# K by two queues, two batches in a nine-row layout, and paired 64-token tails in a linear-attention and expert kernel

## The chip, the cores and the metric

The kernel runs on one core of one Trainium2 chip. A time is the device time of one execution in microseconds (us); the figure quoted for a kernel is the median of its runs. A ratio is the mean time of one kernel's fast runs over that of the other's fast runs of the same rounds, so it is not quite the ratio of the two medians beside it.

Stage times below are taken from one profiled execution of each kernel. They locate a difference; whether a kernel is faster is decided by the timed runs.

## The reference

Eight batches of eight heads, 576 tokens, 64 values a head, all float32. The attention output becomes the 4608 x 512 input of a two-layer block.

```python
def phi(x):
    return np.where(x > 0, x, np.exp(x) - 1.0) + 1.0
q_p, k_p = phi(q), phi(k)
kv  = np.einsum('bhsd,bhse->bhde', k_p, v)
z   = np.sum(k_p, axis=2)
num = np.einsum('bhsd,bhde->bhse', q_p, kv)
den = np.einsum('bhsd,bhd->bhs', q_p, z)[..., None] + 1e-06
x   = (num / den) as (tokens, 512)
h   = x @ w_in                      # 512 -> 2048
g   = h / (1 + exp(-beta * h))
out = g @ w_out                     # 2048 -> 512
```

## The kernel before

TensorE's order is fixed by hand. A batch has an "h" stage (products with w_in), then a "y" stage (products with w_out), and the attention of a later batch is placed between those products. 576 tokens are four groups of 128 and a tail of 64; the eight tails are processed together as a ninth group at the end.

Batch 0 uses another layout: 64 partitions for heads 0 to 3, 64 for heads 4 to 7, nine tokens in each row, so it has no special tail. It is loaded by halves of the partitions:

```python
def load_nine(dst, src, h0=0, h1=HH, j0=0, j1=N9):
    for g in range(2):                       # one transfer for each half of the rows
        nc.gpsimd.dma_start(out=dst[g * TAIL : (g + 1) * TAIL, ...], in_=src[0, ...])
```

All other batches are loaded by a transfer to all 128 partitions, in packets of 512 bytes, and a small one for the tail:

```python
def load_rows(dst, src, b, eng=nc.gpsimd):
    eng.dma_start(out=dst[:, :, 0:NJ, :]..., in_=src[b, :, 0:MAIN, :]...)
    eng.dma_start(out=dst[0:TAIL, :, NJ, :], in_=src[b, :, MAIN:S, :]...)
```

GpSimd issues the transfers in program order; the order after w_in, and the y stage of batch 0:

```python
load_w_out(0); load_w_out(1)
load_k(1); load_q(1)
...                                          # attention of batch 0
load_w_out(2); load_v(1); load_w_out(3)
...
y_phase_wide(0, {
    4: [F(load_next, 3)],
    9: [F(kv_mm, 1), F(kv_evac, 1), F(w_out_scale, 3)],   # K^T V of batch 1
    10: [F(q_trans, 1, 0, 1, wide=True), F(q_trans, 1, 2, 3, wide=True)],
    11: [F(num_mm, 1, 0), F(num_norm, 1, 0)],
    ...                                      # cut
})
```

Later, Q of batch 2 is transposed by a DMA (`q_trans_dma(2)`).

## Time and profile before

| | before |
|---|---|
| time, median (3 runs) | 297.17 us (296.59 to 297.41) |
| profiled span | 295.1 us |
| TensorE busy | 283.9 us, 96% |
| y stage of batch 0, from its first product to the first of the next stage | 34.16 to 52.53 us: 18.37 |
| y stage of batch 1, likewise | 67.61 to 85.25 us: 17.64 |

A row of the timeline has the start, the busy time, engine, source line, operation, output and input, shapes and count; the bracket has the idle time just before and what ended it. A row of the stretches' table has the stretch and its length, busy time (and instruction count) of PE, PEld, DVE, ACT and POOL, then the granted TensorE clock (0.50 is half clock), the DMA share (the packets' own time over that of 16 engines) and GB/s. GB/s counts the bytes written. Of the names, vaug is V with columns of ones, kv_bd holds K^T V, q_pT is the transposed phi(Q), xs the normalized attention and xT its transpose. w_out lands as float32 in the space of xqk, xT and g, hence "xT<-in_moe_w_out_dram", and DVE then scales it. The prediction below shows the main lines of before. Its stretches while the weights and batch 1 are loaded:

```profile
28.00:32.00 4.00, 4.00 (x21) 1.75 (x18) 2.50 (x6) 2.75 (x4) 2.38 (x3) 1.00 1.50 205
...
40.00:44.00 4.00, 3.72 (x54) 1.89 (x54) 3.31 (x3) 2.99 (x3) 2.34 (x4) 1.00 1.21 321
```

And GpSimd's issue of the second transfer of V of batch 1 in its timeline:

```profile
30.20 0.89 POOL L76 DMA_DIRECT2D vraw<-in_v_dram  x1 [0.19 <-issue]
```

### The profile page before, as it was taken

Reading aid. Unit: us, or ns where it says so; the run is one execution under the profiler, and the core shown is the slowest. Engines: PE = TensorE matmul, PEld = TensorE weight load, DVE = VectorE, ACT = ScalarE, POOL = GpSimd, SP = SyncE. Lnnn points to the kernel's source line nnn. Section 1 sums busy time; section 2 is a strip of 40 time slices with the busy share of each in tenths; the row PEclk is TensorE's granted clock in tenths of the full one; section 3 lists DMA queues with packets and bytes.
Section 4 is the critical chain, followed back from the end, with each engine's and each line's share of the span. In section 5 each row is a group of like instructions: output and inputs, shape, how many; then the busy total and the mean of one; then the engine's idle time right before and its main releaser. Section 6 shows DMA issues by size and latency. Waiting matters only on the chain.

```text
span 295.1 us, 4750 instructions
## 1 busy us (share of the span) xinstructions
PE 283.9 (96%) x1891; PEld 143.9 (49%) x1912; DVE 124.0 (42%) x261; ACT 175.1 (59%) x234; POOL 52.7 (18%) x72
## 2 busy tenths in 40 slices
PE   8879999999999999999999999999999999999994
PEld 3557445644465544445444544454445444444444
DVE  4765488504365174616461646154715400110012
ACT  2788786889988780778087907790770077018500
POOL 8924474540003200330023000000000000000000
PEclk9999999999999999999999999999999999999999
DMA  7999999999637993699369945024502400120032
GB/s 103 196 207 343 256 272 192 256 193 192 89 142 100 175 131 113 130 174 154 98 129 159 159 109 124 2 71 116 127 0 72 118 36 0 38 90 16 0 73 71
DMA packets 72310, 37.09 MB, mean 126 GB/s; under 512 B 40912, under 2 KB 66784, under 8 KB 72288
## 3 DMA queue, kind: packets, MB, share of 16 engines
q0 software_dynamic: 38912, 20.45, 47.9%
q1 hardware_dynamic: 33216, 16.20, 22.9%
q8 instruction: 15, 0.25, 0.3%
q10 hardware_dynamic: 160, 0.13, 0.2%
q14 instruction: 7, 0.06, 0.1%
HBM read 36.71 MB, written 9.44 MB: 156 GB/s over the span
## 4 chain that ended last, share of the span: by engine, by line
PE 76%; DMA 9%; POOL 4%; ACT 4%; issue 4%; DVE 1%; ACTq 0%; POOLq 0%; DVEq 0%
PE mm L453 37%; PE mm L505 33%; DMA xT<-in_moe_w_out_dram 5%; DMA vraw<-in_v_dram 4%; PE att L399 3%; ACT e L229 2%; POOL xqk L131 1%; PE att L344 1%; PE mm L537 1%; POOL w_in L159 1%; ACT L229 1%; POOL vraw L131 1%; ACT g L445 1%; DVE qk_p L242 0%; POOL xqk L111 0%
## 5 line engine op out<-in xcount | busy, mean ns | idle before, releaser
L445 ACT ACTIVATE g<-mm,beta_c 128x512 bf16<-128x512 f32 (+2 forms) x156 | 97.3, 633 | 88.4 <-PE mm L453 88.1
L505 PE MATMUL mm<-w_out,g 128*128 128x512 bf16 x541 | 126.7, 379 | 1.2 <-issue 0.3
L453 PE MATMUL mm<-xT,w_in 128*128 128x512 bf16 (+2 forms) x560 | 108.1, 349 | 1.4 <-DMA w_in<-in_moe_w_in_dram 1.1
L453 PEld LDWEIGHTS <-w_in 128*128 128x128 bf16 x656 | 61.9, 98 | 62.4 <-DMA w_in<-in_moe_w_in_dram 1.2
L505 PEld LDWEIGHTS <-g 128*128 128x128 bf16 x560 | 53.0, 98 | 58.2
L515 DVE COPY y_sb<-mm 128x512 f32<-128x512 f32 x27 | 18.7, 691 | 70.6 <-PE mm L505 69.1
L229 ACT ACTIVATE e<-xqk 128x2560 bf16<-128x2560 bf16 x14 | 31.9, 2329 | 0.1
L415 DVE TENSOR_TENSOR xs<-att,rden 128x512 bf16<-128x512 f32 (+1 forms) x40 | 27.6, 689 | 1.4
L242 DVE TENSOR_TENSOR qk_p<-r,e 128x2560 bf16<-128x2560 bf16 x14 | 20.9, 1490 | 13.1 <-ACT e L229 12.4
L355 DVE CAST kv_bd<-att 64x130 bf16<-64x130 f32 x28 | 8.2, 292 | 32.2 <-PE att L344 31.8
L72 POOL DMA_DIRECT2D vraw<-in_v_dram x7 | 6.4, 909 | 84.2 <-DVE vaug L370 78.5
L413 DVE TENSOR_SCALAR den<-att 128x8 f32<-128x8 f32 (+1 forms) x40 | 6.5, 161 | 32.0 <-PE att L399 31.9
L399 PE MATMUL att<-kv_bd,q_pT 128*128 128x130 bf16 (+1 forms) x160 | 15.8, 221 | 1.1 <-DVE kv_bd L370 0.7
L399 PEld LDWEIGHTS <-q_pT 128*128 128x128 bf16 (+1 forms) x160 | 11.6, 100 | 10.7 <-DVE xs L415 2.4
L453 PE MATMUL mm<-xT_tail,w_in 128*128 128x512 bf16 x63 | 13.9, 379 | 0.1
L237 DVE TENSOR_SCALAR r<-xqk 128x2560 bf16<-128x2560 bf16 x14 | 11.6, 834 | 3.8 <-DMA xqk<-in_q_dram 2.3
L575 PE MATMUL mm<-g 128*128 128x512 bf16 x34 | 9.9, 452 | 1.2 <-DVE g L143 1.2
L229 ACT ACT_TABLE_LOAD x7 | 9.0, 1283 | 0.1
L414 DVE RECIPROCAL rden<-den 128x8 f32<-128x8 f32 (+1 forms) x40 | 8.1, 202 | 1.4
L72 POOL DMA_DIRECT2D xqk<-in_k_dram x7 | 6.9, 984 | 6.3 <-DMA w_in<-in_moe_w_in_dram 2.8
L76 POOL DMA_DIRECT2D xqk<-in_k_dram x7 | 7.4, 1057 | 1.5 <-DMA w_in<-in_moe_w_in_dram 1.3
L256 ACT ACTIVATE e<-xqk 128x1280 bf16<-128x1280 bf16 (+1 forms) x4 | 4.4, 1155 | 5.4 <-DMA xqk<-in_k_dram 5.3
(71 smaller groups left out, 140.0 us busy)
## 6 DMA issues: line engine op xcount, KB each, us to landing
out_dram<-y_sb SPq DMA_DIRECT2D x28, 256.0 KB, 2.3
xqk<-in_k_dram POOLq DMA_DIRECT2D x7, 512.0 KB, 10.7
xqk<-in_q_dram POOLq DMA_DIRECT2D x7, 512.0 KB, 11.3
vraw<-in_v_dram POOLq DMA_DIRECT2D x7, 512.0 KB, 11.3
w_in<-in_moe_w_in_dram POOLq DMA_DIRECT2D x4, 512.0 KB, 11.0
g<-in_moe_w_out_dram POOLq DMA_DIRECT2D x4, 512.0 KB, 10.9
out_dram<-y_sb SPq DMA_DIRECT2D x14, 128.0 KB, 5.2
xqk<-in_moe_w_out_dram POOLq DMA_DIRECT2D x2, 512.0 KB, 14.4
```

Source lines behind the costliest of these rows:

```text
L72: eng.dma_start(out=dst[:, :, 0:NJ, :].rearrange("p h j d -> p h (j d)"), in_=src[b, :, 0:MAIN, :].rearrange("h (p j) d -> p h (j d)", j=NJ),)
L229: nc.scalar.activation(st[b, "e", a][:, h0:h1], xqk[b % NX][:, a, h0:h1], ACTF.Exp)
L237: nc.vector.tensor_scalar(st[b, "r", a][:, h0:h1], xqk[b % NX][:, a, h0:h1], 0.0, 1.0, ALU.max, ALU.add)
L242: nc.vector.tensor_tensor(st[b, "p"][:, a].rearrange("p j (h d) -> p h j d", h=H)[:, h0:h1], st[b, "r", a][:, h0:h1], st[b, "e", a][:, h0: ...
L355: nc.vector.tensor_copy(kv_bd[b % 2][i][gs, :, g, :], st[b, "kvp"][gs, 2 * i : 2 * i + 2, :])
L399: nc.tensor.matmul(nps[:n, p // 2, c0 : c0 + 2 * (D + 1)], st[b, "qT"][:, t, p, :n], kv_bd[b % 2][p // 2][:, p % 2], start=True, stop=True ...
L415: nc.vector.tensor_mul(xs[:n], nv[:, :, :, 0:D], rden[:n, :, :, None].to_broadcast([n, 2, 4, D]))
L445: nc.scalar.activation(g_sb[b % 2][:, ff, c0:c1], hp[:, c0:c1], ACTF.Silu, scale=beta_c[:, ff : ff + 1],)
L453: nc.tensor.matmul(hp[:, c0:c1], w_in_sb[ff // 4][:, kc, (ff % 4) * P : (ff % 4 + 1) * P], x[:, t0:t1, kc, :] if b < B else x[:, kc, c0:c1 ...
L505: nc.tensor.matmul(yp, g_sb[b % 2][:, ff, t * P : (t + 1) * P], w_out_sb[ff // 4][:, ff % 4, :], start=(ff == 0), stop=(ff == FC - 1),)
L515: nc.vector.tensor_copy(y_sb, yp)
L575: nc.tensor.matmul(st["warm"], g_sb[0][:, FC - 1, 0:P], g_sb[0][:, FC - 1, :], start=True, stop=True, skip_group_check=True,)
```

## The change

The intent: bring the first K sooner by letting SP issue a part of it (as float32, into space that is free by then); give batch 1 the nine-row layout as well, so that batches 0 and 1 have no tails inside the attention; multiply the tails of two batches in one step, each on one half of TensorE's columns; and transpose all tails of x by DMA rather than by TensorE. The core of the diff:

```diff
-    load_nine(k9, k)
-    load_nine(q9, q, j1=4)
+    load_nine(k_last, k, 0, KF, N9, eng=nc.sync)          # K, columns 5 to 8, float32
+    load_nine(x9[0][1][:, :, 0:KF], k, 0, 0, KF)
+    load_nine(x9[0][0][:, :, 0:QF], q, 0, 0, QF)
 ...
-    load_k(1)
-    load_q(1)
+    load_nine(x9[1][1], k, 1)
+    load_nine(x9[1][0], q, 1)
 ...
-    load_v(1)
+    load_nine(v9[1], v, 1)
 ...
     def num_mm(b, t):
-            nc.tensor.matmul(nps[:n, ...], st[b, "qT"][:, t, p, :n], kv_bd[b % 2]...)
+            for i in range(1 if t < NJ else 2):
+                bb, n, r0 = (b, P, 0) if t < NJ else (b - 1 + i, TAIL, i * TAIL)
+                nc.tensor.matmul(nps[r0 : r0 + n, ...], st[bb, "qT"]..., kv_bd[bb % 2]...)
 ...
-        if by_dma(b):
+        if by_dma(b) or t == NJ:
             nc.sync.dma_start_transpose(out=x_dst(b, t), in_=xs...)
 ...
-    warm(10); beta_trans(); make_beta(); warm(20)
+    warm(10); beta_trans(); warm(15)                        # make_beta later
 ...
-        9: [F(kv_mm, 1), F(kv_evac, 1), F(w_out_scale, 3)],
+        9: [F(kv1), F(w_out_scale, 3)],                     # nine-row form of the same
 ...                                                         # cut: batch 2's x copies to DVE, stores
```

## The prediction

> **What bounds the kernel now.** I read the page's totals first, then a table of the stages, then the timeline inside the stages. The stages are cut where TensorE changes from products with w_in ("h") to products with w_out ("y"). In this table the first number after the stretch is its length, the second is TensorE's busy time, and GB/s is what all DMA engines moved.
>
> ```profile
> PE 283.9 (96%) x1891; PEld 143.9 (49%) x1912; DVE 124.0 (42%) x261; ACT 175.1 (59%) x234; POOL 52.7 (18%) x72
> ...
> 0.00:17.16 17.16, 13.23 (x143) 6.42 (x144) 11.11 (x35) 9.60 (x13) 13.02 (x26) 1.00 1.06 157
> 17.16:33.94 16.78, 16.35 (x151) 11.21 (x152) 9.54 (x23) 13.87 (x32) 7.93 (x10) 1.00 1.28 263
> 33.94:52.53 18.59, 17.64 (x147) 9.42 (x149) 13.86 (x29) 13.69 (x15) 10.69 (x13) 1.00 1.43 249
> 52.53:67.60 15.07, 15.07 (x97) 8.62 (x96) 3.39 (x7) 13.11 (x22) 6.95 (x6) 1.00 1.48 224
> 67.60:85.25 17.65, 16.31 (x126) 8.14 (x128) 7.90 (x18) 17.00 (x17) 0.00 (x0) 1.00 0.89 135
> 85.25:101.41 16.16, 16.16 (x138) 9.36 (x137) 7.86 (x13) 12.66 (x24) 4.69 (x6) 1.00 0.93 137
> 101.41:116.50 15.09, 14.98 (x83) 7.34 (x84) 7.16 (x18) 7.80 (x5) 0.00 (x0) 1.00 0.87 142
> 235.80:263.40 27.60, 27.50 (x127) 12.50 (x128) 2.77 (x4) 10.99 (x16) 0.00 (x0) 1.00 0.10 39
> ```
>
> The row 235.80:263.40 holds nothing but 128 products of 512 columns (one record is missing): 27.60/128 = 0.2156 us each, the full pace. Nine groups of 512 tokens cost 9 x 27.6 = 248 us, which the change doesn't touch. What is left of 295.1 us is 47: 17.2 us of start, about 3.8 at the end, and some 26 of attention products and gaps inside the stages. TensorE's own order is the bound from 17 us on; DVE and ACT matter only where they open a gap in it. So each stage's worth is "its products at full pace, plus gaps". A y stage has 13.8 us of main products. The stages at 33.94 and 67.60 take 18.59 and 17.65, so that is where gaps are.
>
> The timeline shows them, each with what ended it:
>
> ```profile
> 7.49 3.16 ACT L256 ACTIVATE e<-xqk 128x1280 bf16<-128x1280 bf16 x3 [5.25 <-DMA xqk<-in_k_dram]
> ...
> 17.16 1.07 PE L453 MATMUL mm<-xT,w_in 128*128 128x128 bf16 x16 [1.10 <-DMA w_in<-in_moe_w_in_dram]
> ...
> 43.23 0.82 PE L344 MATMUL att<-vaug,qk_p 128*64 128x65 bf16 x40 [0.28 <-DVE vaug L370]
> ...
> 45.75 0.62 PE L380 MATMUL att<-identity,qk_p 128*128 128x128 bf16 x8 [0.28 <-DVE kv_bd L355]
> ...
> 79.33 0.41 PE L399 MATMUL att<-kv_bd,q_pT 128*128 128x130 bf16 x4 [0.34 <-DMA q_pT<-qk_p]
> ...
> 83.07 0.38 PE L433 MATMUL att<-identity,xs 128*128 128x128 bf16 x4 [0.61 <-ACT xT L372]
> ...
> 140.70 0.25 PEld L399 LDWEIGHTS <-q_pT 128*64 128x64 bf16 x4 [0.42 <-DVE xs L415]
> 140.70 0.42 PE L399 MATMUL att<-kv_bd,q_pT 128*64 128x130 bf16 x4
> 141.05 4.86 PEld L505 LDWEIGHTS <-g 128*128 128x128 bf16 x24
> ```
>
> See that K arrives at 7.5; that the first h product waits 1.1 us for w_in, not for x, whose copy (DVE, 15.88 for 0.42 us) ended at 16.30; that batch 1 waits for V and for bank release, batch 2 for an ACT copy; and that a 64-token tail holds TensorE from 140.70 to 141.05, 0.35 us, where a full group of 128 tokens takes 0.23 (138.65 to 138.88).
>
> **What the skill says.** (1) "DMA: Bandwidth & Descriptors", section "Issuing engines are not separate DMA queues": transfers from different issuers share the same 16 engines, and a second issuer saves only issue time. The trace agrees for 4 us on: the share is 1.15 and more there. But K's first packet starts at 2.73, while the beta row's, issued on SP, starts at 1.82 (packet records), so SP can fill an idle 0.9 us. (2) Same page, "SWDGE vs HWDGE vs iDMA": a cast needs GpSimd's queue, so the SP part of K arrives as f32. (3) "VectorE: DVE Perf Modes", "The perf-mode tier table": tensor_scalar is half as fast from f32 SBUF as from bf16. The trace agrees: 128x512 from f32 took 0.44 us, 128x2560 from bf16 0.83. (4) "TensorEngine Tiling (Array Packing)", "Performance Considerations": columns up to 64 permit two halves. The trace's 40 products of 128*64 by 65 columns occupy 43.23 to 43.98 = 19 ns each, against 65/512 x 0.2156 = 27 ns for a lone one: halves do overlap.
>
> **The change, part by part.** Counts of TensorE instructions are from both programs' instruction order.
>
> K by two queues. Per packet, K's 1152-byte writes took a median 107 ns (512 packets, 32 per engine: 3.4 us from 2.73); 640-byte ones 69 ns (2.2 us); SP's own 1024-byte output packets about 46 ns (1.5 us). New: SP starts at about 1.85, does 0.9 us alone, its last 0.6 interleaves, so K's engine time ends at 2.73 + 2.2 + 0.6 = 5.5 in place of 6.1 (an estimate; the slowest engine lags a further 1 us in both). Everything queued behind, w_in too, comes 0.6 earlier. x gains the same less 0.2 us for the f32 relu and still precedes w_in; beta's five small DVE operations (1.1 us) move into a wait for TensorE (1.5 us at 11.4 to 12.9). First h product at about 16.55: **-0.6**.
>
> Stage 17.16 (h of batch 0): its tail products (0.35) and its four 64-wide transposes (0.22) go: **-0.57**.
>
> Stage 33.94 (y of 0, attention of 1): K^T V in 36 products of 64 rows by 130 columns in place of 40; their like at L307 took 1.19 us for 36 of 128 columns, so about 1.05 against 0.75, +0.3. Q's transposes become 32 of 64x64 (16 took 0.41 with drain; about 0.75 against 0.9), -0.15. V of batch 1 comes in 512 packets of 1152 bytes in place of 1024 of 512 and 512 of 128: 3.4 us per tensor in place of 4.9 (64 x 60 + 32 x 32 ns per engine); K, Q and V of batch 1 together 4 us earlier, so the waits of 0.28 at 43.23 (V) and, with Q's banks taken as one tile, 0.28 + 0.2 at 45.75 go; of 1.6 us of gaps I keep 0.9, because the second product of the group now waits for three ACT copies (2.2 us). Net **-0.5**.
>
> Stage 52.53 (h of 1): tail products now 8, for both batches; at half overlap 0.45 against 0.35; transposes of the tail (0.22) go to DMA: **-0.15**.
>
> Stage 67.60 (y of 1, attention of 2): the x copies go from ACT to DVE, which is 45% busy there, and the second transposes move four products later. The gap at 83.07 (0.61 by the row, 0.78 between neighbours' ends) goes, that at 79.33 stays: **-0.8**.
>
> Stage 85.25 (h of 2): tail products and transposes go (0.57), and a part of the small gaps beside them: **-0.7**.
>
> Batches 3 to 7: tails of 4 and 6 vanish (0.35 + 0.09 before each: -0.88); 3, 5 and 7 do pairs (+0.1 each): **-0.6**.
>
> Sum: 0.6 + 0.57 + 0.5 + 0.15 + 0.8 + 0.7 + 0.6 = 3.9. 297.17 - 3.9 = **293.2 us**. The end (last store at 290) is the same work.
>
> **Rivals.** (a) The two column halves do not overlap when the weights differ per batch: then a pair costs 0.70, four pairs lose 4 x 0.25, and the time is 294.2. For it: each 64-column product costs 88 ns where a full one costs 58, so a weight load shows. Against it: the 19 ns above. (b) K's two queues only share: DMA is saturated from 3.5 us, packets rise by 512, and the fixed part of a packet, some 24 ns, costs 512 x 24/16 = 0.77 us, as much as the early start gives. Then the start gains nothing and the result is 293.8. For it: share over 1. Against: SP's packets are shorter than GpSimd's of like size. (c) In the stage at 33.94 DVE becomes the bound: it gets a memset pair of 0.75 us (0.48 + 0.27) before the kv copies and more ones to set; together some 0.95 us. If phi of Q isn't early, the products at 47.07 wait up to 0.7 longer: 293.9. (d) The other way: an early V lets all gaps of that stage close and w_in's slowest engine (last packet 1 us behind the mean) gains from K's part without GpSimd's ring: 1.5 us more, 291.7.
>
> **Range and chances.** Losses (a) to (c) all together give 295.3; gain (d) 291.7, with the 0.2 us spread of runs. 8 in 10: 291.5 to 295.1. Faster by 2% needs 291.2 or less, 6 us of gain where I can point at 3.9 and (d)'s 1.5: 0.08. Slower by 2% has no mechanism here: 0.01.
>
> **What would show it.** Right: first exp near 6.9 and first h product near 16.5, still waiting for w_in; no TensorE wait for V in batch 1; the wait for an ACT copy of xT gone; pairs of tails occupying 0.4 to 0.5 us; the steady y stage of even batches at 14.7, odd ones at 15.2. Wrong: a pair at 0.7 us (a), first h product still at 17.1 (b), TensorE waiting for kv_bd or xs of batch 1 longer than before (c). The prediction fails if the start moves over 1.5 us, or the stages at 33.94 and 67.60 keep their gaps.

## More of the kernel before

Experiments were timed in four sittings (on chips that the record numbers 15, 11, 11 and 14), each with its own runs of the kernel before, whose medians were 296.4 to 296.7 us. Ratios, not medians, are compared across sittings.

## The result, and the profile after

| | before | after |
|---|---|---|
| time, median (4 runs each) | 296.96 us (296.59 to 297.41) | 298.38 us (298.27 to 298.58) |
| ratio of fast runs | | 1.0048 (95%: 1.0031 to 1.0065) |
| profiled span | 295.1 | 296.5 |

The change is half a per cent slower, where a gain of 3.9 us was predicted: "within 2%", as predicted, but outside the range. The stage table of the changed kernel, with cuts at the same places as in the prediction's table of before:

```profile
0.00:16.43 16.43, 12.78 (x138) 6.23 (x140) 9.25 (x30) 8.98 (x12) 14.09 (x27) 1.00 1.10 176
16.43:32.63 16.20, 15.77 (x143) 10.97 (x143) 7.47 (x20) 13.96 (x32) 4.45 (x8) 1.00 1.17 267
32.63:56.48 23.85, 19.31 (x160) 9.78 (x162) 15.45 (x35) 13.33 (x16) 12.69 (x16) 0.93 1.35 225
56.48:71.34 14.86, 14.86 (x97) 8.53 (x96) 3.46 (x7) 12.91 (x21) 4.64 (x6) 1.00 1.45 222
71.34:88.17 16.83, 16.30 (x126) 8.10 (x128) 8.60 (x20) 15.91 (x15) 0.00 (x0) 1.00 0.83 97
88.17:103.55 15.38, 15.38 (x130) 9.00 (x130) 7.68 (x12) 11.67 (x21) 4.69 (x6) 1.00 1.01 163
```

Every row but the third is shorter than its partner before. The third, the y stage of batch 0 with batch 1's attention, is 23.85 us where it was 18.59. It is also the only one whose clock is not 1.00.

The start of each stage, from TensorE's first product in it:

| stage starts at | before | after | change within the stage before it | predicted |
|---|---|---|---|---|
| h of 0 | 17.16 | 16.43 | -0.73 | -0.6 |
| y of 0 | 34.16 | 32.85 | -0.58 | -0.57 |
| h of 1 | 52.53 | 56.48 | **+5.26** | -0.5 |
| y of 1 | 67.61 | 71.35 | -0.21 | -0.15 |
| h of 2 | 85.25 | 88.17 | -0.82 | -0.8 |
| y of 2 | 101.19 | 103.33 | -0.78 | -0.7 |
| end | 295.08 | 296.50 | -0.72 | -0.6 |

So one stage took all the gain and 1.4 us more. TensorE's timeline in that stage, with a pair of tails (112.98) from later on:

```profile
45.76 1.21 PE L342 MATMUL att<-vaug,qk_p 64*128 64x130 bf16 x36 [3.25 <-DVE vaug L362]
47.12 1.35 PE L548 MATMUL mm<-w_out,g 128*128 128x512 bf16 x3 [0.16 <-issue]
...
49.38 1.66 PE L548 MATMUL mm<-w_out,g 128*128 128x512 bf16 x4
...
112.98 0.42 PE L440 MATMUL att<-kv_bd,q_pT 128*64 128x130 bf16 x8
113.33 5.35 PE L548 MATMUL mm<-w_out,g 128*128 128x512 bf16 x24
```

TensorE stood for 3.25 us waiting for the copy of V of batch 1, against 0.28 before. Right after it, three products of 512 columns took 1.35 us and four took 1.66, about twice the 0.2156 each: the clock record has half clock from 47.25 to 50.67 us. A wait of 0.70 us for w_out at 40.62 adds to it. The pair of tails holds TensorE from 112.98 to 113.33, 0.35 us, as long as a single tail did.

DVE's timeline says why V was late:

```profile
32.07 0.88 DVE L214 TENSOR_SCALAR w_out<-xT,rbeta 128x512 bf16<-128x512 f32 x2 [1.99 <-DMA xT<-in_moe_w_out_dram]
...
44.94 0.76 DVE L362 COPY vaug<-vraw 128x2304 bf16<-128x2304 bf16 x1 [0.77 <-DMA vraw<-in_v_dram]
```

V is copied at 44.94 where it was 41.91, and w_out's second quarter is scaled at 32.07 where it was 29.94; both waited for a transfer. The chain of waits links the two:

```profile
13.94 18.11 DMA xT<-in_moe_w_out_dram
32.33 12.51 DMA vraw<-in_v_dram
```

The second half of V is issued only when that quarter of w_out has landed:

```profile
32.33 0.77 POOL L136 DMA_DIRECT2D vraw<-in_v_dram  x1 [2.10 <-DMA xT<-in_moe_w_out_dram]
```

In both kernels GpSimd's rows show the same habit: it issues a transfer once the one eight places before it has landed. Before, that cost V's second transfer no wait on a DMA (0.19, issue); now it cost 2.10 us. So the question is why a transfer of w_out, which the change doesn't touch, lands 2 us later. In the packet records, its last 4096-byte packets (after 28.3 us) took 165 to 172 ns each before, and 256 to 472 ns now. Meanwhile the stream as a whole:

```profile
28.00:32.00 4.00, 4.00 (x21) 1.78 (x19) 1.08 (x3) 2.61 (x5) 1.10 (x2) 1.00 1.22 200
...
40.00:44.00 4.00, 1.89 (x8) 0.68 (x7) 2.87 (x5) 1.59 (x3) 2.00 (x2) 1.00 1.07 270
```

At 28 to 32 us, while K and Q of batch 1 are loaded, it moves as many bytes as before (200 against 205 GB/s), at a smaller share (1.22 against 1.50). In the mixed stretch at 40 it moves 270 where it was 321.

### The profile page after: what moved, and what is told of

It reads as the page before. It is cut to its first block, busy times and chain, and to the rows that moved or that the text cites. A ratio compares the mean times of both kernels' runs of the same rounds, so it can differ in the third digit from the quotient of the medians.

```text
span 296.5 us, 4735 instructions
## 1 busy us (share of the span) xinstructions
PE 282.6 (95%) x1886; PEld 143.0 (48%) x1907; DVE 120.4 (41%) x254; ACT 171.9 (58%) x227; POOL 50.0 (17%) x72
## 4 chain that ended last, share of the span: by engine, by line
PE 82%; DMA 10%; POOL 4%; DVE 2%; issue 1%; POOLq 0%; DVEq 0%
PE mm L548 37%; PE mm L494 36%; DMA xT<-in_moe_w_out_dram 6%; DMA vraw<-in_v_dram 4%; PE att L440 3%; PE att L382 2%; POOL xqk L136 1%; PE mm L580 1%; PE att L494 1%; POOL w_in L161 1%; POOL vraw L136 1%; DVE xs L456 1%; POOL xqk L111 0%; PE att L342 0%; PE att L295 0%
## 5 line engine op out<-in xcount | busy, mean ns | idle before, releaser
L231 ACT ACTIVATE e<-xqk 128x2560 bf16<-128x2560 bf16 x12 | 27.4, 2328 | 0.1
L456 DVE TENSOR_TENSOR xs<-att,rden 128x512 bf16<-128x512 f32 x36 | 24.9, 692 | 1.2
L244 DVE TENSOR_TENSOR qk_p<-r,e 128x2560 bf16<-128x2560 bf16 x12 | 17.9, 1493 | 12.8 <-ACT e L231 12.1
L454 DVE TENSOR_SCALAR den<-att 128x8 f32<-128x8 f32 x36 | 5.9, 163 | 27.7 <-PE att L440 27.5
L440 PE MATMUL att<-kv_bd,q_pT 128*128 128x130 bf16 (+1 forms) x160 | 14.1, 221 | 0.7 <-DVE kv_bd L408 0.4
L268 ACT ACTIVATE e<-xqk 128x1280 bf16<-128x1280 bf16 (+2 forms) x5 | 7.7, 1562 | 5.4 <-DMA xqk<-in_k_dram 5.4
L410 ACT ACTIVATE q_pT<-att 128x512 bf16<-128x512 bf16 (+2 forms) x8 | 4.9, 652 | 9.1 <-PE att L295 9.1
L239 DVE TENSOR_SCALAR r<-xqk 128x2560 bf16<-128x2560 bf16 x12 | 9.7, 819 | 0.0
L455 DVE RECIPROCAL rden<-den 128x8 f32<-128x8 f32 x36 | 7.3, 203 | 1.2
L494 PE MATMUL att<-xT,w_in 128*128 128x512 bf16 x32 | 7.2, 379 | 0.0
```

Of the source, the lines that this page charges most:

```text
L231: nc.scalar.activation(st[b, "e", a][:, h0:h1], xqk[b % NX][:, a, h0:h1], ACTF.Exp)
L239: nc.vector.tensor_scalar(st[b, "r", a][:, h0:h1], xqk[b % NX][:, a, h0:h1], 0.0, 1.0, ALU.max, ALU.add)
L244: nc.vector.tensor_tensor(st[b, "p"][:, a].rearrange("p j (h d) -> p h j d", h=H)[:, h0:h1], st[b, "r", a][:, h0:h1], st[b, "e", a][:, h0: ...
L268: nc.scalar.activation(st[b, "e", a][:, j0:j1].rearrange("p j h d -> p h j d"), in9(b, a, j0, j1), ACTF.Exp,)
L440: nc.tensor.matmul(nps[r0 : r0 + n, p // 2, c0 : c0 + 2 * (D + 1)], st[bb, "qT"][:, t, p, :n], kv_bd[bb % 2][p // 2][:, p % 2], start=True ...
L455: nc.vector.reciprocal(rden[:n], den[:n])
```

## The experiments

The first theory was that batch 1's nine-row layout, by its transfers, makes V late, and that V's lateness is the whole loss. Rivals were the half clock, K's two queues, and the order of V and w_out.

### Batch 1 in the layout of before

The rest of the change stays.

```diff
-    load_nine(x9[1][1], k, 1); load_nine(x9[1][0], q, 1)
+    load_k(1); load_q(1)
-    load_nine(v9[1], v, 1)
+    load_v(1)
     # and exp, relu, phi, K^T V, Q's transposes and stores of batch 1 as before
```

> Only batch 1 is put back to the 128-partition layout with its 64-row tails; K by two queues, batch 0 without a tail, paired tails and DMA transposes stay. Theory T1 (the 64-partition loads of batch 1 slow the DMA stream): V of batch 1 lands near 41.5 us again in place of 44.9, TensorE's 3.25 us wait before batch 1's K^T V shrinks to 1.3 or less, the clock does not fall to half, and the time is 293 to 294.5 us. Theory T2 (the early f32 K on SP, or the issue order, is what delays V): V still lands near 44 and the time stays within 0.7 us of 298.4.

Measured: 298.0 us (296.26 to 298.13), ratio 1.0040 (1.001 to 1.007). TensorE's timeline:

```profile
42.55 0.82 PE L384 MATMUL att<-vaug,qk_p 128*64 128x65 bf16 x40 [1.15 <-DVE vaug L410]
...
81.54 0.62 PE L442 MATMUL att<-kv_bd,q_pT 128*128 128x130 bf16 x4 [3.43 <-DMA q_pT<-qk_p]
81.95 1.91 PE L550 MATMUL mm<-w_out,g 128*128 128x512 bf16 x4
```

V came back to 41.67 us, and the h stage of batch 1 starts at 51.86, 4.6 us before the changed kernel. Half of the theory holds. But the time hardly moved, because a second wait appeared in the next stage: TensorE stood 3.43 us for the transposed Q of batch 2 and then ran at half clock for 3.41 us (four products in 1.91). So V's lateness had hidden another loss. The first row shows a third thing: V lands when it landed before the change (41.67 against 41.91), so TensorE, which comes earlier, waits longer (1.15 against 0.28). The 1.5 us gained up to the y stage's start shrink to 0.67 at the next.

### Work for TensorE during the wait

```diff
         kvp = att_banks()
+        st["warm"] = kvp[:, 0]
+        warm(14)                    # fourteen idle products while V comes
         kv_mm9(...)
```

> The changed kernel with 14 filler products of 512 columns (14 x 0.216 = 3.0 us) put where TensorE waits for V of batch 1. If the 3.41 us at half clock that the trace shows after that wait is due to the idleness, the clock stays at 1.00 and the time falls by about half of 3.4 us, to 296.7 us; the wait itself stays. If the half clock has another cause, the time stays at 298.4 or gets worse.

Measured: 298.3 us, ratio 1.0071 (1.0048 to 1.0094). The half clock at 47 us was gone (in the profiled run it now lay at 11.76 to 15.17), and K^T V started at 45.60 instead of 45.76. One of its runs had a mean clock of 1.000 and still took 298.36, where 296.7 was expected. The stage became 1 us shorter in the profile (33.61 to 56.22), but only because it began 0.76 us later; it ended 0.26 earlier. Taking the half clock at 47 us away doesn't bring the time back.

The traces show why. From the start of K^T V to the next stage TensorE needs 9.30 us in the kernel before and 10.72 in the changed kernel; here, at full clock, it still needs 10.62. Three other runs with batch 1 in the nine-row layout and no half clock there (K by one queue, and both runs with four transfers of 64 rows, below) need 10.71 or 10.72. At full clock TensorE waits for DVE instead; DVE's timeline, then TensorE's:

```profile
46.87 0.48 DVE L92 MEMSET xqk<- 64x512 uint32 x1 [0.16 <-issue]
```

```profile
51.26 0.38 PE L548 MATMUL mm<-w_out,g 128*128 128x512 bf16 x1 [0.33 <-DVE w_out L214]
...
52.42 0.40 PE L474 MATMUL att<-identity,xs 128*128 128x128 bf16 x4 [0.56 <-DVE xs L456]
```

In the nine-row layout DVE clears tail rows (two memsets, 0.48 and 0.27 us) before it copies K^T V, so that copy starts 2.04 us after K^T V where it was 1.26, and all that follows on DVE is later. So some 1.4 us of the loss come with the nine-row layout, whatever the clock does, and the waits point to its work on DVE. No run takes the memsets away alone, so that cause is argued, not shown.

### K by one queue

```diff
-    load_nine(k_last, k, 0, KF, N9, eng=nc.sync)
-    load_nine(x9[0][1][:, :, 0:KF], k, 0, 0, KF)
+    load_nine(x9[0][1], k, 0)                # and the beta row goes back to SP
```

> The changed kernel with K of batch 0 by GpSimd's queue alone again. If two queues are worth the 0.7 us by which the first h product came earlier (16.43 against 17.16), that product goes back to about 17.1; and as the wait for V of batch 1 is set by the same DMA stream, V lands some 0.4 us later and the time is 298.6 to 299.2. If K's two queues are themselves what delays V (T2), V lands earlier than 44.9 and the time falls below 298.

Measured: 297.92 us, ratio 1.0051 (1.0032 to 1.0071), the same as the whole change. Whether K comes by two queues makes no difference that these runs can see. V's copy began at 44.19 us, 0.75 earlier, and the median is a little under 298, which by the letter are T2's signs; but the ratio has not moved (1.0051 against 1.0048), and V is still 2.3 us later than before. The first h product came at 17.12, as expected, but in this profile a half-clock window (12.60 to 16.01) lay ahead of it. TensorE still waited 2.83 us for V (45.01 us), here without a half-clock window after it.

### V ahead of a quarter of w_out

```diff
-    load_w_out(2)
     load_nine(v9[1], v, 1)
+    load_w_out(2)
     load_w_out(3)
```

> The changed kernel with V of batch 1 issued before the third quarter of w_out. T1 with a stream bound by its rate: V lands near 40 and that quarter near 44 in place of 41.6, so TensorE waits for w_out instead (it reaches it at 39.9) and the time changes by less than 1 us. If only V's place in the queue was wrong, the time falls by 3 us or more.

Measured: 298.53 us, ratio 1.0066 (1.0045 to 1.0087).

```profile
42.92 3.22 PE L548 MATMUL mm<-w_out,g 128*128 128x512 bf16 x8 [1.97 <-DVE w_out L214]
46.78 1.21 PE L342 MATMUL att<-vaug,qk_p 64*128 64x130 bf16 x36 [0.64 <-DVE vaug L362]
```

The wait for V fell to 0.64 us and that for w_out rose to 1.97. V itself landed at about 41 us (its last packet ended at 40.67), near the 40 that was expected; its copy stood behind the scaling of w_out in DVE's order until 45.80. The order only chooses who waits.

### The rows of a transfer: a failed try

The Trainium skill, "SBUF — State Buffer", section "Door 1: The DMA port swizzle (why [64,N] ≈ [32,N])", says that a transfer to 64 partitions reaches 8 of the memory's 16 ports. The next two runs were to tell this from the packet's length. The first has transfers to all 128 rows, the second has as many transfers to 64 rows.

```diff
+    for h in range(HH):                       # run 1: one head of each half, 128 rows
+        nc.gpsimd.dma_start(out=dst[:, h]..., in_=src[b].rearrange("(g h) (p j) d -> h g p (j d)", ...)[h])
```

> The changed kernel, but K, Q and V of batch 1 come in four transfers each that write 1152-byte packets to all 128 partitions (one head of each half a transfer), in place of two transfers each to 64 partitions. Same bytes, same packets, same layout. Theory A (transfers to 64 partitions use the memory badly, so the stream slows and V is late): V of batch 1 lands near 42 us, TensorE's wait for it falls from 3.25 us to under 1.3, the first h product of batch 1 starts at 52 to 53.5 instead of 56.5. Theory B (the 1152-byte packets, or the number of transfers allowed under way, make V late): V still lands at 44 to 46 us or later, since there are now more transfers of which each must wait for the one eight before it, and the wait stays above 2.5 us.

> The control of the run before: K, Q and V of batch 1 in four transfers each as there, of the same 1152-byte packets and the same bytes, but each to 64 partitions (two heads of one half). Theory A (64 partitions): V lands at 44.5 us or later as in the changed kernel, TensorE waits 3 us or more, and this run is slower than the other. Theory B (packets or number of transfers): this run and the other agree within 0.5 us in V's landing.

Measured: 304.26 us for the 128 rows (ratio 1.0303, 1.0225 to 1.0380) and 296.75 for the 64 (1.0006, 0.9982 to 1.0030). In the first, TensorE waited 2.15 us for w_out and 5.83 for V; in the second V's copy began at 42.86 and the wait was 1.55 us. Read as they were written, both expectations are against the theory of the rows (the second's Theory B failed too: V's copies were 7 us apart). But the first run is no test. Its stream moved 110 GB/s at 28 to 30 us, and some 1460 packets of 4 bytes ran from 28 to 29 us, where other runs have at most some twenty in a microsecond. Its source pattern has the two halves as the outermost dimension. The skill, "DMA: Bandwidth & Descriptors", section "Rules for kernel authors", says that an outermost dimension shorter than 16 confines a transfer to at most as many engines. No record here names a packet's engine, so that stays a probable cause. What the second run shows is that four smaller transfers in place of two, which alternate between the halves, halve the wait. It also shows that V's late issue is not by itself what makes V late. GpSimd's timeline in the second run:

```profile
33.60 2.52 POOL L146 DMA_DIRECT2D vraw<-in_v_dram  x4
```

All of V was issued there after the changed kernel had issued its last part (32.33), and V still came 2.1 us earlier (42.86 against 44.94).

### Shorter packets to 64 rows

```diff
-    load_nine(x9[1][1], k, 1)
+    load_nine(x9[1][1][:, :, 0:4], k, 1, 0, 4)       # 512-byte packets
+    load_nine(x9[1][1][:, :, 4:N9], k, 1, 4, N9)     # 640-byte packets; Q and V likewise
```

> The changed kernel, but K, Q and V of batch 1 come in packets of 512 and 640 bytes (token columns 0 to 3, then 4 to 8), four transfers a tensor to 64 partitions each, in place of 1152-byte packets. Same bytes, layout and rows. The run with four transfers of 1152-byte packets to 64 partitions is its control: there V's copy began at 42.86 us, TensorE waited 1.55 us for it, and the last 4096-byte packets of w_out took 244 to 368 ns beside the 1152-byte ones, where they take 165 to 172 in the kernel before. Theory P (the long packets hold up the w_out packets that run beside them, and that delays V): the last w_out packets before 30 us take under 200 ns, V's copy begins at 42.2 or earlier, and the wait is 1.3 us or less. Theory R (writing to 64 partitions at a time does it, whatever the packet): they still take over 240 ns and V's copy begins at 42.8 or later.

Measured: 297.26 us, ratio 1.0023 (1.0003 to 1.0044). V's copy began at 42.90 us and TensorE waited 1.49 us, as good as equal to the run with 1152-byte packets in as many transfers (42.86 and 1.55). The last w_out packets took 233 to 328 ns (a little under Theory R's 240 at the low end). Between these two runs the packet's length made no difference to V.

### The rows alone

Batch 1 in the layout of before, with 512-byte packets, only in two transfers of 64 rows instead of one of 128:

```diff
-    load_k(1); load_q(1)
+    load_halves(xqk[1][:, 1], k, 1); load_halves(xqk[1][:, 0], q, 1)
+    # load_halves: dst[0:64], then dst[64:128]; the tail as before. V likewise
```

> The first experiment (batch 1 in the standard layout, 512-byte packets), in which only the rows of a transfer are changed: the 512-token part of K, Q and V of batch 1 comes in two transfers of 64 partitions each in place of one of 128. In the first experiment the last 4096-byte packets of w_out before 30 us took 165 to 173 ns, V's copy began at 41.67 us and TensorE waited 1.15 us for it. Theory R (writing 64 partitions at a time holds up the w_out packets that run beside it): those packets take over 230 ns, V's copy begins at 42.7 or later, and the wait is 2 us or more. Rival (it is the layout of nine, its addresses in memory, and not the rows): the packets stay under 180 ns and V's copy begins before 42.2.

Measured: 299.86 us, ratio 1.0111 (1.0073 to 1.0150). TensorE's timeline, then DVE's:

```profile
45.50 0.82 PE L396 MATMUL att<-vaug,qk_p 128*64 128x65 bf16 x40 [3.28 <-DVE vaug L422]
```

```profile
31.41 0.88 DVE L228 TENSOR_SCALAR w_out<-xT,rbeta 128x512 bf16<-128x512 f32 x2 [1.82 <-DMA xT<-in_moe_w_out_dram]
...
44.62 0.83 DVE L422 COPY vaug<-vraw 128x2560 bf16<-128x2560 bf16 x1 [0.79 <-DMA vraw<-in_v_dram]
```

This is the changed kernel's picture again, in the old layout: a wait of 3.28 us (3.25 there), V's copy at 44.62 (44.94), and w_out's last packets at 286 to 458 ns beside 165 to 173 in the run with 128 rows. Against that run, only the halving of the rows (and with it one more transfer a tensor) was changed. More transfers do not explain it: with four to a tensor V came earlier in the two runs above. So it is the rows, with one reserve: the added transfers also shift GpSimd's order, and V was issued at 32.66 to 35.2 us here, 28.79 to 31.0 with 128 rows. The skill's rule on ports is the likely reason; what is shown is the effect. The stream alone is no slower: at 30 to 32 us, when no w_out packet runs, it moves 186 GB/s here and 187 with 128 rows. It is the other transfer's packets, running beside it, that take about twice as long. That holds in every profile: 182 to 520 ns in the seven runs whose batch 1 comes by 64 rows, 165 to 173 in the six that load it by 128 rows in the old layout. How far V's copy is then late differs, though: 2.3 to 3.0 us with two or three transfers a tensor, 1.0 with four (the run with V ahead of w_out left out).

### The tails' transposing transfer

Now the second wait, found in the first experiment. There the packet records had the 256-byte packets of the tails' transposing transfer at 58 to 61.5 us, amid the loads (batch 4's were queued behind). The table of stretches of before, then of that run:

```profile
58.00:62.00 4.00, 4.00 (x20) 1.77 (x19) 0.00 (x0) 2.98 (x5) 1.56 (x2) 1.00 1.53 208
...
74.00:78.00 4.00, 3.84 (x54) 2.07 (x48) 1.17 (x4) 3.97 (x4) 0.00 (x0) 1.00 0.92 155
78.00:82.00 4.00, 3.54 (x25) 1.65 (x23) 2.09 (x6) 3.97 (x5) 0.00 (x0) 1.00 0.00 0
```

```profile
58.00:62.00 4.00, 4.00 (x21) 1.76 (x19) 0.00 (x0) 3.12 (x6) 1.13 (x2) 1.00 1.57 152
...
74.00:78.00 4.00, 4.00 (x20) 1.66 (x17) 0.91 (x4) 3.99 (x3) 0.00 (x0) 1.00 1.43 143
78.00:82.00 4.00, 0.57 (x6) 0.46 (x6) 0.00 (x0) 3.14 (x3) 0.00 (x0) 0.93 0.43 65
```

The loads lose (208 - 152) x 4 us = 224 KB at 58, and the stream, empty at 78 before, still runs there. Q's transposing transfer, issued at 69.41, landed 12.1 us later; before it took 9.0. To test it, the first pair of tails is transposed by TensorE again:

```diff
-        if by_dma(b) or t == NJ:
+        if by_dma(b) or (t == NJ and b > 1):
+            3: [F(x_trans, 1, 4)],
```

> The first experiment, but the tail pair of batches 0 and 1 is transposed by TensorE as before the change, not by a transposing transfer. There the packets of that transfer ran at 58 to 61.5 us, in which time the loads moved 150 GB/s in place of some 210, and the loads of batch 4 ended at 78 us in place of 75. Theory (that transfer holds up the loads, and these the next transposing transfer): the loads end 1.5 to 2 us earlier, TensorE's wait at 81.5 us falls from 3.43 to 1.0 to 2.0 us, the half-clock window after it may go, and the time is 1.5 to 3 us lower than in that experiment less 0.2 us for the TensorE transposes. Rival (the loads are late for another reason): the wait stays above 3 us.

Measured: 294.50 us (294.32 to 294.88), ratio 0.9932 (0.9913 to 0.9951). The stretch 58 to 62 us moves 226 GB/s, Q's transfer lands 8.1 us after its issue, and TensorE doesn't wait for it. (Its profiled run had half clock from 11.34 to 18.16 us and so came 2.9 us later to the first h product, which hides some of the wait; its run at a mean clock of 1.000 took 294.32, so the gain isn't owed to that.) The wait had been expected to shrink to 1 to 2 us; it went altogether. One transposing transfer of 128 KB, put where it looked free, cost some 3.2 us (ratio 1.0040 against 0.9932, of 296.5 us).

### Holding back the loads

The other side of the same meeting: the loads of batch 4 wait for a small GpSimd copy that reads Q of batch 2.

```diff
+    def late_loads():
+        nc.gpsimd.tensor_copy(gate, st[2, "p"][:, 0, 0, 0:2])    # Q written, its transfer issued
+        load_next(4)
```

> The first experiment (batch 1 in the standard layout) with one thing more: the loads of batch 4 are held back by a small GpSimd copy until Q of batch 2 has been written, so that the transposing transfer of Q of batch 2 does not run among them. There TensorE waited 3.43 us for that transfer at 81.5 us and then ran 3.41 us at half clock. Theory (the loads delay the transposing transfer): the transfer lands within 7 us of its issue in place of 12.1, the wait falls under 0.4 us, no half-clock window near 81 us, and the time falls to 293 to 294.5 us. Rival (the transfer takes 9 to 12 us by itself, or waits for something else): the wait stays above 1.5 us and the time stays within 1 us of 298.

Measured: 294.99 us (294.35 to 297.12), ratio 0.9959 (0.9918 to 1.0001). The wait fell from 3.43 to 1.73 us only and the transfer landed 10.4 us after its issue: the half clock went and the time fell, but the theory's three figures were missed, and of the rival's two signs one held (a wait over 1.5 us). A version with everything put together, released at the same point, and with K^T V of batch 1 four products later, was the next try:

> A version meant to beat both kernels: the first experiment (batch 1 in the standard layout) with the first tail pair transposed by TensorE, the loads of batch 4 held back until Q of batch 2 is written, K^T V of batch 1 one group of four products later (it waited 1.15 us for V), and 20 warm-up products in the second block in place of 15. If the three waits that the experiments showed are the cause: no TensorE wait over 0.5 us after 20 us, and 292 to 293.8 us. If the waits only move: 294 to 295 us, as the run with the tail pair on TensorE alone (294.5).

Measured: 295.59 us (294.80 to 297.00), ratio 0.9970 (0.9944 to 0.9996): no better, and the expectation failed.

```profile
80.34 0.40 PE L442 MATMUL att<-kv_bd,q_pT 128*128 128x130 bf16 x4 [1.81 <-DMA q_pT<-qk_p]
```

The packet records say why: the transposing packets ran alone from 71 us, but the loads began at 74, and the last few of the transfer's packets ran among them until 78; in the run before, its data packets had ended by 74.6, but its 4-byte packets ran only at 77.6 to 78.7. Putting K^T V later only swapped the wait for V (0.60) for one on phi of Q (0.58) and one on kv_bd (0.49), so that part was taken back. The last version releases the loads when the transfer has landed:

```diff
-        nc.gpsimd.tensor_copy(gate, st[2, "p"][:, 0, 0, 0:2])
+        nc.gpsimd.tensor_copy(gate, st[2, "qT"][:, 0, 0, 0:2])   # the transposed Q
```

> The version meant to beat both kernels, mended: batch 1 in the standard layout, K^T V of batch 1 at its place of before, the first tail pair transposed by TensorE, 20 warm-up products, and the loads of batch 4 held back until the transposing transfer of Q of batch 2 has landed, not only until it is issued. In the two runs that released them at its issue TensorE waited 1.73 and 1.81 us for that transfer, whose last packets ran among loads that began at 74 us. Theory (the transfer's end is held up by loads that begin before it has landed): it lands within 7 us of its issue in place of 10.4, TensorE waits for it under 0.4 us, and the time is 292.8 to 293.8 us. Rival (the transfer needs 9 us or more by itself): the wait stays above 1.2 us, and the time at 294.5 to 295.5 us.

Measured: **293.49 us** (293.25 to 293.79), ratio **0.9888** (0.9872 to 0.9905), against 296.70 for before in the same rounds. TensorE's timeline:

```profile
42.87 0.82 PE L384 MATMUL att<-vaug,qk_p 128*64 128x65 bf16 x40 [0.87 <-DVE vaug L410]
...
78.61 1.02 PE L550 MATMUL mm<-w_out,g 128*128 128x512 bf16 x4
```

The transfer landed 5.0 us after its issue (within 7 was expected), no idle time stands before the products at 78.61, and the h stage of batch 2 starts at 83.82 instead of 85.25. The mean clock was 0.999 or more in all its runs. It beats both kernels. What is left there is the wait of 0.87 us for V.

## Why the prediction was wrong

**The step that failed** is "Stage 33.94", and in it "K, Q and V of batch 1 together 4 us earlier". That sum added the packets' durations and divided by 16 engines. It is wrong twice. An engine has more than one packet in flight (the share was 1.50 before and 1.22 after at the same 200 GB/s or so), so packet times don't add up to stream time; and between the runs with long and with short packets their length made no difference. What it left out is that the new transfers write 64 rows at a time. That held up w_out's last packets, and V's copy came 3.0 us later (44.94 against 41.91) instead of 4 earlier. The late issue of V behind w_out is a part of how, but not shown to be all: in the run with transfers in fours V was issued later still and came earlier. The stage, in place of -0.5, measured +5.26: the wait for V is 2.97 of it, that for w_out 0.70, and 1.42 lie between K^T V and the next stage (10.72 us against 9.30). This last part is not owed to the half clock, since runs at full clock have it too (10.62 to 10.72). It points to rival (c). The skill's page with the rule on ports was not drawn on in the prediction, although the change's diff is full of transfers to 64 partitions.

**A second step failed unseen.** In "Stage 52.53" the tail's transposes "go to DMA: -0.15", as if a transfer cost nothing. The stage did gain 0.21. But where V is on time, this transfer makes the loads late and these make Q's transposing transfer late, in the next stage: taking it back was worth about 3.2 us (ratio 1.0040 to 0.9932). In the changed kernel itself this cost is hidden, because TensorE came 3.7 us later than before into that stage.

**A third point was the sum itself.** The gains before batch 1's K^T V were counted as gains of the whole. The stage at 33.94 waits for V, whose time is set by the stream and not by TensorE. With the old layout V came at 41.67, and 1.5 us gained upstream became 0.67.

**What held.** The other stages came within 0.13 us of their terms: -0.73, -0.58, -0.21, -0.82, -0.78 and -0.72 for a predicted -0.6, -0.57, -0.15, -0.8, -0.7 and -0.6. Not all of that is foresight: in the stage at 67.60 the gap at 79.33, which was to stay, went as well, because TensorE came 3.7 us later. Rival (a) is refuted: a pair of tails takes 0.35 us, so the halves overlap fully, better than the "half overlap" in the sum. Of rival (b), the mechanism that was predicted did not show: the first exp starts at 7.59 us, not near 6.9 (before 7.49), and with K by one queue the time is the same. In the profiled run the first h product no longer waited for w_in; in the run with 64-row transfers in fours it waited 1.19 us again, with the same K loads. So the 0.73 of the start isn't shown to be K's, and its nearness to 0.6 may be luck. The early start itself was smaller than reckoned: SP's first packet of K ran at 2.30 us, not 1.85, and GpSimd's at 3.29, where it was 2.70 before; K's last packet ended at 6.68 in place of 7.10. Rival (c), DVE, is not behind the two long waits, which end with a transfer. But the memset pair that it names does run before the kv copies, and what follows K^T V takes 1.4 us longer, where (c) had 0.7; in the changed kernel's own profile the half clock hides it. So (c) came true in part, as far as the traces show. The rival that happened, transfers that become slower for others, was not on the list. Rival (d) saw V early; it was late.

Two small slips in the recorded text: its losses (a) to (c) add up to 295.5 us, not 295.3; and its two DVE durations differ by 2.6 times per column (0.44 us for 512 and 0.83 for 2560), so they agree with "half as fast" only roughly.

That the last version takes 293.49 us, near the estimate of 293.2, does not confirm the sum: it drops two parts of the change and has one that the prediction didn't, the held-back loads.

## What to carry to other kernels

Before a transfer is reshaped, ask how many rows it writes and what else is in flight: a transfer to half of the rows may be as fast by itself and still delay its neighbours, and the first thing that waits for a neighbour pays. A transposing transfer isn't free because it leaves TensorE: keep it out of a stretch in which loads must drain, and keep loads off it until it has landed. When a profile's wait hides behind a larger one, undo the larger one alone and look again before summing gains.

## What the Trainium skill lacked or had wrong

- "SBUF — State Buffer", on ports: it gives the bandwidth of a lone transfer to 64 partitions and of two such at once. Here the stream by itself lost nothing (186 GB/s against 187). The cost fell on another transfer beside it, whose 4096-byte packets took 286 to 458 ns instead of 165 to 173; for such a mixture the page has no figure.
- "DMA: Bandwidth & Descriptors", on DMA Transpose: no figure for what loads and a transposing transfer do to each other. Here loads fell to 152 GB/s from 208 for 4 us, and in the worst microsecond (59 to 60) 512-byte packets took a mean of some 130 ns instead of 60. Q's transfer took 5.0 us from issue to landing with no loads beside it, 8.1 to 12.1 among them.
- The same page, "Rules for kernel authors": two transfers to halves of the partitions are discouraged because they serialize. The runs show a further reason: ratio 1.0111 against 1.0040 for the same data in the same layout.
- "TensorE: Matmul & The Clock Gate", "What's actually happening": half clock is said to come after an idle window of about 3.4 us. Here it came with a wait of 3.43 us, but also with shorter ones of 3.25, 3.28 and 1.97, and not with 2.83 or 1.81; each time it lasted 3.41 us.
- No page found has the order of issue on GpSimd that held V back (a transfer is issued once the one eight places before it has landed: 2.10 us of waiting for V's second half). Whether the chip or the program sets it isn't shown.
